# Windowed attention with a mixture of experts on one core: half of a slot's row split and one weight split moved into the next step, the slot's rows requested ahead of a step's last loads, a quarter of some q and k loads issued from GpSimd

## The chip, the cores and the metric

One core of a Trainium2 chip runs the whole kernel. The time is device microseconds of one execution; three runs of the kernel before gave 609.14, 609.82 and 610.5 us, median 609.82. The engines are TensorE (PE, with its weight loads PEld), VectorE (DVE), ScalarE (ACT), GpSimd (POOL) and SyncE (SP, which here only issues DMAs). Each engine runs its own instructions in the order in which the program wrote them, and waits where one depends on another engine.

## The reference

The inputs are q, k and v of shape (8 batches, 8 heads, 576 positions, 64), the weights of 8 experts and a gate. Attention sees a causal window of 64 positions; its output becomes 4608 rows of 512, and each row goes to one expert.

```python
scores = scale * np.matmul(q, k.transpose(0, 1, 3, 2))
scores = np.where((rel >= 0) & (rel < 64), scores, -1e9)   # rel = pos_q - pos_k
attn = exp(scores - max); attn /= attn.sum() + 1e-9
x = (attn @ v) as rows of 512
logits = x @ w_gate + modality_bias[modality_id]
e_idx = argmax(logits); gate_w = softmax(logits)[e_idx]
out[mask] = gate_w[mask] * (relu(x[mask] @ w1[e]) @ w2[e])    # for each expert e
```

## The kernel before, in words

**Steps.** The attention is worked off in 36 pieces of 128 rows (two blocks of 64), one step `s` each, in the loop at line 1080 that runs to `s` = 39. A step holds several stages of different pieces: `values(s - 2)` (probabilities times v, and on DVE `values_out`, which divides by the sums and writes `xa`, L726), `logits(s - 3)` (the gate's matmuls, L744, and the addition of the bias on DVE, L749, which also frees the PSUM bank), `scores(s)` (L659), `minima(s)` (eight DVE instructions that mask and take the row's minimum, L673), the transposing of the probabilities of piece `s - 1` on PE with copies on ACT (`probs_t`, L694), the exponentials on ACT (`exps`, L685, in three groups: two, three and three of the eight heads), the transposing of `xa` for the gate (`x_t`), the routing, and `part(0)` and `part(1)`, which bring the next group's q or k into transposed form.

**Order.** The schedule is manual: instructions stand on each engine in the order of the program. Work that is to stand a little later is appended to the list `later`, and `run_later()` empties it.

**Slots of the experts.** Rows whose expert is known are scattered to `xs_scratch` in HBM by GpSimd (L828). From step 12 on, slots of 256 rows of one of two chosen experts are computed between the attention's stages: a generator, `slot_pieces`, yields one piece of work after the other, and `gap` takes one. A slot has 16 pieces and a step takes four, so a slot lasts four steps. The pieces are twelve for k = 1 to 3 (two of `first`, x times w1, L321; two of `second`, h times w2, L343), then `second(3, 0)` of the old slot, `first(0, 0)` and `first(0, 1)` of the next one, and `second(3, 1)` of the old one. With the slots beginning at step 12, these last four lie in the steps with s % 4 == 0 (16, 20, 24, 28, 32, 36).

**A slot's rows.** In the fourth gap of a step with s % 4 == 2 `fetch` reads the slot's row number into SP's register (L204) and asks for the rows with five DMAs on SP (L217); they must wait for the scatters that write these rows. A step later, behind the second gap, `x_turn` transposes them on DVE (two instructions, L283). Then the rows are split into a high part (`xh`, cast on ACT, L195) and a remainder (`xl`, subtraction on DVE, L196), in two halves: `x_part(nxt, 0)` and `x_part(nxt, 1)`. `x_part` itself emits no work: it appends the split, and for the second half also two small GpSimd copies (gate and id, L304 and L306), to `later`. Before the change both are emitted at the end of the step with s % 4 == 3, around the last piece of that step. Each group of `first` has 12 matmuls: the first six use the first half of the channels, the last six the second, and the remainder `xl` is used last in each six.

**Weights.** The two experts' weights come in 32 pieces of 256 KB, from step 5 to about step 25. `weights(s)` splits the remainder of the piece before (`split_lo` on DVE, L119), casts the next piece's high part (`split_hi` on ACT, L114), and asks SP for another piece (L103, L107).

**Loads of q and k.** `load_qk` issues one group's loads. In the groups of `WHOLE` (10, 12, 14, 16, 17) every head goes directly to the layout that DVE transposes (`turn_heads`, L585): per head two DMAs of 32 KB, each of 32 rows with 8 runs of 128 bytes. k of group G is loaded in step 2G - 3 and transposed in step 2G - 2, q one step later each. Of these DMAs, a quarter (odd heads, second half) is issued from ACT's queue, the rest from SP's (L608): 40 in all, 20 of k and 20 of q. In a step the loads are called in four places: `loads(3)`, `loads(1)`, `loads(1)` and at the end `loads(9)`, which takes what is left; in a `WHOLE` group that is the last two heads. `loads(9)` stands ahead of the fourth gap, hence of `fetch`.

**GpSimd.** In a step it copies the lower half of v (`swap_v`, L551), which `values` needs a step later, adds the small number to the sums (L700), scatters two pieces of rows in every second step, and scatters a finished slot's output (L354).

Of the kernel before, what the change touches and what calls it, by code (L numbers as in the profile page):

```python
# [26 lines left out]
def tile_window_attn_moe(  # L27
# [12 lines left out]
    nc = tc.nc  # L40
# [88 lines left out]
    def tick(n=1, table=False):  # L129
        for _ in range(n):  # L130
            if routing and not table:
                routing.pop(0)()
            elif queue:
                queue.pop(0)()
                issued[0] += 1
# [105 lines left out]
    RAWS = 8  # L241
    fetched = []
    later = []
    scattered = []

    n_tps = [0]
# [14 lines left out]
    def run_later():  # L261
        while later:
            later.pop(0)()
# [21 lines left out]
    def slot_pieces():  # L285


        def x_part(sl, i):

            xt, nb = sl["xt"], sl["nb"]  # L290
            if nb == 1:
                return
            if i == 0:
                sl["x"] = [epool.tile([P, NC1 * TP], F32R, name=nm) for nm in ("xh", "xl")]
            cs_ = slice(2 * i, 2 * i + 2)
            raw = x_of(xt).rearrange("p b w c t -> p c (b w) t")[:, cs_]
            hi, lo = (x[:, cs_.start * TP:][:, 0:512].rearrange("p (c w t) -> p c w t", w=2 * NR, t=R32)
                      for x in sl["x"])

            def out_():  # L300
                split(raw, hi, lo)
                if i == 1:
                    sl["gate"] = epool.tile([P, 2], F32, name="gate", bufs=2)
                    nc.gpsimd.tensor_copy(out=sl["gate"], in_=tail_of(xt)[:, :, 0])  # L304
                    sl["id"] = epool.tile([P, 2], I32, name="id", bufs=2)
                    nc.gpsimd.tensor_copy(out=sl["id"], in_=tail_of(xt)[:, :, 1])  # L306
            later.append(out_)
# [118 lines left out]
        while True:  # L426
            nxt = None
            for k in range(1, NK):
                for i in range(2):
                    if k == 1 and i == 0 and last:  # L430
                        nxt = fetch()
                        turn_at = 0
                    first(sl, k, i)
                    if k == NK - 1 and i == turn_at:
                        later.append(lambda: x_turn(nxt))
                    yield
                for t in range(2):
                    if k == 2 and t == 1 and nxt is None:
                        nxt = fetch()
                        turn_at = 1  # L440
                    second(sl, k - 1, t)
                    if k == NK - 1 and nxt and t == 1 and nxt["nb"] == 2:
                        x_part(nxt, 1)
                    yield
                    if k == NK - 1 and nxt and t == 0:
                        x_part(nxt, 0)
                        run_later()
            if nxt["nb"] == 1:
                break
            second(sl, NK - 1, 0)  # L450
            yield
            first(nxt, 0, 0)
            yield
            first(nxt, 0, 1)
            yield
            second(sl, NK - 1, 1)
            yield
            sl = nxt
# [130 lines left out]
    def load_qk(G, nm, blocks=range(GBLK), dma=nc.sync, hs=range(H)):  # L589

        t = qk[G, nm]
        x = q if nm == "q" else k
        nh = n_plain(G)
        i = blocks[0]
        while i <= blocks[-1]:
            b, g = divmod(GBLK * G + i, BPB)
            n = min(BPB - g, blocks[-1] + 1 - i)
            p0 = i * W64 // 2
            for par in range(2 if hs[0] < nh else 0):
                src = x[b, 0:nh, g * W64:(g + n) * W64].rearrange("h (p t) d -> p t h d", t=2)  # L600
                dma.dma_start(out=plain(t, nh)[p0:p0 + n * W64 // 2, par], in_=src[:, par])  # L601
            u = slice(i * W64 // R32, (i + n) * W64 // R32)
            for h in hs if hs[0] >= nh else ():
                for c in range(2):
                    rows = slice((h % 2 * 2 + c) * R32, (h % 2 * 2 + c + 1) * R32)
                    src = x[b, h, g * W64:(g + n) * W64, c * R32:(c + 1) * R32]
                    other = nh == 0 and h % 2 and c
                    (nc.scalar if other else dma).dma_start(  # L608
                        out=by_heads(t, nh)[rows, (h - nh) // 2, u, :],
                        in_=src.rearrange("(u p) d -> p u d", p=R32))  # L610
            i += n
# [108 lines left out]
    def values_out(p):  # L720
        rs = st.pop((p, "rs"))
        rw = small.tile([P, 2, 2, HP], F32, name="rw")
        nc.vector.reciprocal(
            out=rw, in_=rs.rearrange("p (c g) -> p g c", g=2)[:, :, None, :].broadcast_to([P, 2, 2, HP]))
        xa = st[p, "xa"] = xas[p % XBUF]
        nc.vector.tensor_tensor(  # L726
            out=xa[:, 0:DM].rearrange("p (x d) -> p x d", d=R32),
            in0=st.pop((p, "av")).rearrange("p h d -> p (h d)").rearrange("p (x d) -> p x d", d=R32),
            in1=rw.rearrange("p g a c -> p (g a c)")[:, :, None].broadcast_to([P, 2 * H, R32]), op=ALU.mult)
# [334 lines left out]
            out=wg[c * R32:(c + 1) * R32],  # L1064
            in_=w_gate[c * P:(c + 1) * P].rearrange("(r d) e -> d r e", d=R32))

    def weights(s):

        if halves:
            split_lo(*halves.pop(0))  # L1070
        n = 2 if s < FIRST + 4 else 1
        if len(raws) >= n or raws and not pieces:
            split_hi(*raws[0])
            halves.append(raws.pop(0))
        while pieces and len(raws) < n:
            x, c = pieces.pop(0)
            raw = epool.tile([P, WCH], F32, name="y", bufs=4)
            raws.append((load_piece(raw, evs[x], c), x, c))

    for s in range(NPR + 4):  # L1080
# [10 lines left out]
        def loads(n):  # L1091

            for f, args in at.get(s, [])[:n]:
                f(*args)
            at[s] = at.get(s, [])[n:]
# [31 lines left out]
                route1((s - 3) // GB)  # L1127
        if FIRST < s < NPR + 2:
            values_out(s - 2)
        if s < NPR:  # L1130
            scores(s)
            if s == FIRST:
                x_turn(fetched[0])
                gap(it, True)
            minima(s)
            if s == FIRST - 2:
                tick(todo[0][-1] - issued[0], table=True)
# [58 lines left out]
        if s == WEIGHTS:  # L1196
            load_weights()
        if s >= WEIGHTS:
            weights(s)
        if s > FIRST:  # L1200
            loads(9)
        if n_gap > 3:
            gap(it, True)
        run_later()
        if s == 1:
            select_bias()
        if s == 4:
            nc.sync.dma_start(out=xs_blk[DUMMY:DUMMY + 2].rearrange("b p c -> p b c"), in_=padrow)
        for T, xs_ in EARLY:
            if T == R:  # L1210
                plan(T, xs_, cnt)
    tick(len(routing))
    release()
    tick(len(queue))
# [132 lines left out]
    while next(it, "end") != "end":  # L1347
# [20 lines left out]
        if swaps and swaps[0][0] <= t:  # L1368
# [4 lines left out]
            else:  # L1373
                split_hi(raw, buf, c)
                split_lo(raw, buf, c)
    assert not swaps and not todo
    manual.__exit__(None, None, None)
    actx.close()

# [124 lines left out]
```

## Time and profile before

| | |
|---|---|
| runs | 609.14, 609.82, 610.5 us (median 609.82) |
| the profiled execution | 611.84 us, span 610.0 us, granted TensorE clock 0.997 |
| busy: PE, DVE, ACT, POOL | 96%, 62%, 46%, 23% of the span |
| DMA queues: SP's (q1), GpSimd's (q0), ACT's (q10) | 66.02, 18.92 and 1.89 MB |
| steps 12 to 35 (74.5 to 313 us) | PE busy 231.9 of 238.5 us |

The page has the busy time of each engine, the span in 40 slices, the chain of work that ended last and the costliest groups. In a timeline each row has the start, the duration, engine, line, operation, what is written and read, and in brackets the engine's idle time before it and what ended it. `SPq` and `ACTq` are those engines' DMA issues. "x9" is the number of instructions merged in a row. Instructions of one engine overlap by a few hundredths, so the start of the next is where the one before ended, for this purpose.

### The profile page before, as it was taken

How to read it: one execution, taken by the hardware profiler on the slowest of the kernel's cores; microseconds unless marked ns; L12 is line 12 of the kernel's file. 1: busy time of each engine (PE TensorE's matmuls, PEld its weight loads, DVE VectorE, ACT ScalarE, POOL GpSimd, SP SyncE). 2: the span in 40 equal slices, each digit the busy share in tenths (PEclk: the TensorE clock that was granted, in tenths of full speed). 3: DMA queues.
4: the chain of work that ended last, by engine and by line, in shares of the span. 5: the costliest groups of instructions: out<-in, count | busy, mean ns of one | idle time of the engine just before them, and what ended most of it. 6: DMA issues, size and time to landing. Idle time of an engine off the chain costs nothing.

```text
span 610.0 us, 17261 instructions
## 1 busy us (share of the span) xinstructions
PE 588.4 (96%) x6241; PEld 522.5 (86%) x6241; DVE 377.0 (62%) x1479; ACT 282.8 (46%) x907; POOL 138.4 (23%) x313
## 2 busy tenths in 40 slices
PE   7999889999899999999999999999999999999996
PEld 4888788889689898889898899899999999999983
DVE  4889988887767877768756465323224634765311
ACT  3999876665556655555562211111113522553110
POOL 6332322142132312321323131011001111102102
PEclk9999989999999999999999999999999999999999
DMA  9989867685865846554713033632152553687401
GB/s 169 212 226 246 212 180 168 144 196 133 203 155 132 229 88 155 145 107 86 188 54 105 36 105 127 188 102 70 36 174 77 166 174 103 194 255 215 153 23 38
DMA packets 186855, 87.95 MB, mean 144 GB/s; under 512 B 151002, under 2 KB 169488, under 8 KB 186640
## 3 DMA queue, kind: packets, MB, share of 16 engines
q1 hardware_dynamic: 167312, 66.02, 44.8%
q0 software_dynamic: 5840, 18.92, 8.2%
q10 hardware_dynamic: 13616, 1.89, 1.8%
q8 instruction: 50, 0.82, 0.6%
q14 instruction: 37, 0.30, 0.2%
HBM read 67.36 MB, written 23.78 MB: 149 GB/s over the span
## 4 chain that ended last, share of the span: by engine, by line
PE 76%; DVE 9%; DMA 6%; ACT 3%; issue 2%; POOL 2%; SPq 1%; POOLq 0%; DVEq 0%; ACTq 0%
PE y L343 29%; PE em L321 20%; PE sp L321 10%; PE tp L483 6%; PE av L715 4%; PE sp L659 3%; DVE ss L673 2%; DMA qk<-in_k_dram 2%; DMA xs_scratch<-xa,idx 2%; PE tp L744 2%; ACT ss L685 1%; DMA xt<-xs_scratch 1%; DVE xl L196 1%; POOL xs_scratch L828 1%; SPq L601 1%
## 5 line engine op out<-in xcount | busy, mean ns | idle before, releaser
L343 PE MATMUL y<-Whi,hh 128*128 128x512 f32 x288 | 115.8, 402 | 0.0
L685 ACT ACTIVATE ss<-ss,mn 128x128 f32<-128x128 f32 x288 | 112.2, 397 | 3.8 <-DMA wg<-in_moe_w_gate_dram 2.7
L343 PE MATMUL y<-Wlo,hh 128*128 128x512 f32 x288 | 112.7, 391 | 0.0
L343 PE MATMUL y<-Whi,hl 128*128 128x512 f32 x288 | 112.4, 390 | 0.0
L330 DVE SCALAR_TENSOR_TENSOR hl<-em,hh 128x512 fp32r<-128x512 f32 x50 | 34.6, 691 | 91.3 <-ACT hh L329 91.2
L354 POOL DMA_INDIRECT out_dram<-y,id x36 | 38.6, 1073 | 217.7 <-DVE y L351 160.1
L321 PE MATMUL em<-xh,Whi 128*128 128x256 f32 x400 | 82.1, 287 | 0.0
L321 PE MATMUL em<-xh,Wlo 128*128 128x256 f32 x400 | 79.5, 280 | 0.0
L321 PE MATMUL em<-xl,Whi 128*128 128x256 f32 x400 | 79.5, 280 | 0.0
L329 ACT ACTIVATE hh<-em 128x512 fp32r<-128x512 f32 x50 | 29.9, 598 | 105.1 <-PE em L321 100.2
L321 PEld LDWEIGHTS em<-xh,Whi 128*128 128x128 f32 x400 | 63.2, 190 | 2.3
L343 PEld LDWEIGHTS y<-Whi,hl 128*128 128x128 f32 x288 | 54.1, 188 | 12.1
L673 DVE CUSTOM_DVE_ANT_0 ss<-sp,masks 128x128 f32<-128x128 f32 x288 | 63.4, 285 | 1.5 <-PE sp L659 1.5
L694 ACT COPY pT<-tp 128x512 f32<-128x512 f32 x57 | 31.3, 589 | 70.9 <-PE tp L483 70.7
L343 PEld LDWEIGHTS y<-Whi,hh 128*128 128x128 f32 x288 | 54.1, 188 | 9.5 <-issue 0.8
L343 PEld LDWEIGHTS y<-Wlo,hh 128*128 128x128 f32 x288 | 54.2, 188 | 8.5
L321 PEld LDWEIGHTS em<-xl,Whi 128*128 128x128 f32 x400 | 61.4, 189 | 0.0
L321 PEld LDWEIGHTS em<-xh,Wlo 128*128 128x128 f32 x400 | 61.4, 189 | 0.0
L828 POOL DMA_INDIRECT xs_scratch<-xa,idx x36 | 36.3, 1009 | 89.3 <-DVE e_n_p L154 23.5
L685 ACT ACTIVATION_READ_ACCUMULATOR ss<-ss,mn 128x1 f32 x288 | 56.1, 195 | 0.0
L329 ACT ACTIVATE hh<-sp 128x512 fp32r<-128x512 f32 x22 | 13.1, 597 | 80.4 <-PE sp L321 80.4
L715 PEld LDWEIGHTS av<-ve,pT 128*64 128x64 f32 x576 | 36.3, 138 | 13.1 <-issue 6.9
(239 smaller groups left out, 1131.5 us busy)
## 6 DMA issues: line engine op xcount, KB each, us to landing
xt<-xs_scratch SPq DMA_DIRECT2D x72, 128.0 KB
vo<-in_v_dram SPq DMA_DIRECT2D x32, 256.0 KB
y<-in_moe_w_dram SPq DMA_DIRECT2D x32, 256.0 KB
vo<-in_moe_w_dram SPq DMA_DIRECT2D x18, 256.0 KB
ss<-in_moe_w_dram SPq DMA_DIRECT2D x18, 256.0 KB
xs_scratch<-xs_scratch SPq DMA_DIRECT2D x8, 514.0 KB
pT<-in_moe_w_dram SPq DMA_DIRECT2D x12, 256.0 KB
qk<-in_k_dram SPq DMA_DIRECT2D x76, 32.0 KB
```

The costliest lines, as they stand in the source:

```text
L321: nc.tensor.matmul(out=hb[:, i * TP:(i + 1) * TP], lhsT=w[buf][:, c0:c0 + P], rhs=x[:, c * TP:(c + 1) * TP], start=(n == 0), stop=(n == le ...
L329: nc.scalar.activation(out=hh, in_=hb, func=AF.Relu),
L330: nc.vector.scalar_tensor_tensor(out=hl, in0=hb, scalar=0.0, in1=hh.bitcast(F32), op0=ALU.max, op1=ALU.subtract)))
L343: nc.tensor.matmul(out=sl["y", t], lhsT=h[:, i * TP + t * P:i * TP + (t + 1) * P], rhs=w[buf][:, c0:c0 + DM], start=(k == 0 and n == 0), s ...
L354: ins = nc.gpsimd.indirect_dma_start(out=out, out_offset=bass.IndirectOffsetOnAxis(ap=sl["id"][:, t:t + 1], axis=0), in_=y, in_offset=None ...
L483: nc.tensor.transpose(out=out_, in_=in_, identity=ident[p0:p0 + n, p0:p0 + n])
L659: nc.tensor.matmul(out=sp[a][c * W64:(c + 1) * W64, hp * P:(hp + 1) * P], lhsT=qT[rows, place(g + c, hp), :], rhs=kT[rows, win(c, hp), :], ...
L673: nc.vector.tensor_tensor_reduce(out=ss[a][:, hp, :], in0=sp[a][:, hp * P:(hp + 1) * P], in1=mask, scale=-1.0 / 8.0, scalar=3.0e38, op0=AL ...
L685: nc.scalar.activation(out=ss[a][:, hp, :], in_=ss[a][:, hp, :], func=AF.Exp, bias=mn[:, h:h + 1], scale=-1.0, accum_out=sm[:, h:h + 1])
L694: nc.scalar.copy(out=pT, in_=pp)
L715: nc.tensor.matmul(out=by_block(av)[c * W64:(c + 1) * W64, a, :, hp, :], lhsT=pT[:, i:i + W64], rhs=(vo if c else ve)[p][:, 2 * hp + a, :] ...
L828: ins = nc.gpsimd.indirect_dma_start(out=xs, out_offset=bass.IndirectOffsetOnAxis(ap=idx[:, j:j + 1], axis=0), in_=xg[j], in_offset=None)
```

## The change

`x_part(nxt, 1)` is no longer called where the step with s % 4 == 3 ends. It is put into a new list, `splits`, which the next step empties behind `values_out` and ahead of `scores`. In the phase behind the steps (when `last` is set) it is called at once, as before. In steps with s % 4 == 3 beyond step 12 the last call of `weights` puts its `split_lo` into the same list. `loads(9)` stands behind the fourth gap. The quarter of the `WHOLE` groups' loads goes to GpSimd's queue instead of ACT's.

```diff
--- before.py
+++ after.py
@@ -241,6 +241,7 @@
     RAWS = 8
     fetched = []
     later = []
+    splits = []
     scattered = []
 
     n_tps = [0]
@@ -439,8 +440,10 @@
                         nxt = fetch()
                         turn_at = 1
                     second(sl, k - 1, t)
-                    if k == NK - 1 and nxt and t == 1 and nxt["nb"] == 2:
-                        x_part(nxt, 1)
+                    if k == NK - 1 and nxt and t == 1:
+                        splits.append(lambda: x_part(nxt, 1))
+                        if last:
+                            splits.pop(0)()
                     yield
                     if k == NK - 1 and nxt and t == 0:
                         x_part(nxt, 0)
@@ -605,7 +608,7 @@
                     rows = slice((h % 2 * 2 + c) * R32, (h % 2 * 2 + c + 1) * R32)
                     src = x[b, h, g * W64:(g + n) * W64, c * R32:(c + 1) * R32]
                     other = nh == 0 and h % 2 and c
-                    (nc.scalar if other else dma).dma_start(
+                    (nc.gpsimd if other else dma).dma_start(
                         out=by_heads(t, nh)[rows, (h - nh) // 2, u, :],
                         in_=src.rearrange("(u p) d -> p u d", p=R32))
             i += n
@@ -1064,9 +1067,12 @@
             out=wg[c * R32:(c + 1) * R32],
             in_=w_gate[c * P:(c + 1) * P].rearrange("(r d) e -> d r e", d=R32))
 
-    def weights(s):
-
-        if halves:
+    def weights(s, late=False):
+
+        if halves and late:
+            half = halves[0]
+            splits.append(lambda: (halves.remove(half), split_lo(*half)))
+        elif halves:
             split_lo(*halves.pop(0))
         n = 2 if s < FIRST + 4 else 1
         if len(raws) >= n or raws and not pieces:
@@ -1127,6 +1133,8 @@
                 route1((s - 3) // GB)
         if FIRST < s < NPR + 2:
             values_out(s - 2)
+        while splits:
+            splits.pop(0)()
         if s < NPR:
             scores(s)
             if s == FIRST:
@@ -1196,12 +1204,12 @@
         if s == WEIGHTS:
             load_weights()
         if s >= WEIGHTS:
-            weights(s)
-        if s > FIRST:
-            loads(9)
+            weights(s, s > FIRST and s % 4 == 3)
         if n_gap > 3:
             gap(it, True)
         run_later()
+        if s > FIRST:
+            loads(9)
         if s == 1:
             select_bias()
         if s == 4:
@@ -1209,6 +1217,8 @@
         for T, xs_ in EARLY:
             if T == R:
                 plan(T, xs_, cnt)
+    while splits:
+        splits.pop(0)()
     tick(len(routing))
     release()
     tick(len(queue))
@@ -1373,7 +1383,7 @@
             else:
                 split_hi(raw, buf, c)
                 split_lo(raw, buf, c)
-    assert not swaps and not todo
+    assert not swaps and not todo and not splits
     manual.__exit__(None, None, None)
     actx.close()
```

## The prediction

> **What bounds the kernel now.** I read the page first, then the windows by step, the waits of PE between 100 and 330 us (there the change acts), and the timelines of PE, DVE, ACT, SP and POOL around the steps that begin a new slot.
>
> ```profile
> PE 588.4 (96%) x6241; PEld 522.5 (86%) x6241; DVE 377.0 (62%) x1479; ACT 282.8 (46%) x907; POOL 138.4 (23%) x313
> ```
>
> PE lacks 610.0 - 588.4 = 21.6 us of being busy throughout, which caps any gain.
>
> ```profile
> 157.27:171.19 13.92, 11.13 (x141) 9.46 (x137) 11.12 (x44) 8.09 (x26) 5.02 (x11) 1.00 0.79 212
> 201.20:212.93 11.73, 10.90 (x141) 9.47 (x137) 9.67 (x44) 6.92 (x24) 4.57 (x9) 1.00 0.90 237
> 242.96:253.79 10.83, 10.67 (x140) 9.48 (x136) 8.76 (x42) 5.92 (x23) 3.49 (x6) 1.00 0.56 147
> ```
>
> These are steps 20, 24 and 28, each counted from its score matmuls: the stretch, its length, then busy time of PE, PEld, DVE, ACT and POOL. A step with s % 4 == 0 finishes one slot and begins the next. Step 20 leaves PE idle for 2.79 us, step 24 for 0.83, step 28 for 0.16. The waits say who was late:
>
> ```profile
> PE tp L483 <- DVE lg L749: 2.4, 4, 0.9
> PE sp L659 <- DVE qT L585: 1.7, 1, 1.7
> ```
>
> Four times a transposing of probabilities waits for the logits' addition on DVE (it frees the bank), once the scores wait for a transposed q. PE's rows give the places (bracket: idle before):
>
> ```profile
> 119.30 0.66 PE L483 MATMUL tp<-ident_r,ss 128*128 128x128 f32 x4 [0.43 <-DVE lg L749]
> 159.59 0.67 PE L659 MATMUL sp<-kT,qT 64*64 64x128 f32 x16 [1.66 <-DVE qT L585]
> 161.76 0.66 PE L483 MATMUL tp<-ident_r,ss 128*128 128x128 f32 x4 [0.91 <-DVE lg L749]
> 203.50 0.65 PE L483 MATMUL tp<-ident_r,ss 128*128 128x128 f32 x4 [0.61 <-DVE lg L749]
> 323.44 0.66 PE L483 MATMUL tp<-ident_r,ss 128*128 128x128 f32 x4 [0.40 <-DVE lg L749]
> ```
>
> So steps 16, 20, 24 and 36 lose 0.43 + 1.66 + 0.91 + 0.61 + 0.40 = 4.01 us to DVE, and steps 28 and 32 nothing. About 4 us is what the change can reach. Why DVE is late at step 20:
>
> ```profile
> 154.28 0.69 DVE L330 SCALAR_TENSOR_TENSOR hl<-em,hh 128x512 fp32r<-128x512 f32 x1 [0.68 <-ACT hh L329]
> 157.12 1.30 DVE L283 STREAM_TRANSPOSE xt<-xt 128x512 f32<-128x512 f32 x2 [2.15 <-DMA xt<-xs_scratch]
> 158.85 0.69 DVE L585 STREAM_TRANSPOSE qT<-qk 128x512 f32<-128x512 f32 x1
> 159.46 0.96 DVE L119 TENSOR_TENSOR Wlo<-y,Whi 128x512 fp32r<-128x512 f32 x1
> 160.34 1.28 DVE L196 TENSOR_TENSOR xl<-xt,xh 128x512 fp32r<-128x512 f32 x2
> 161.55 0.15 DVE L749 TENSOR_TENSOR lg<-tp,bias_sel 128x8 f32<-128x8 f32 x1
> 164.28 0.42 DVE L557 COPY ve<-vo 64x512 f32<-64x512 f32 x1
> ```
>
> DVE stood 2.15 us waiting for the slot's rows, then ran without a break from 157.12 to 164.70. The rows were late because of SP:
>
> ```profile
> 141.17 7.44 SPq L608 DMA_DIRECT2D qk<-in_q_dram  x9
> 148.85 1.26 SPq L103 DMA_DIRECT2D y<-in_moe_w_dram  x1
> 150.16 1.42 SPq L608 DMA_DIRECT2D qk<-in_q_dram  x3
> 152.53 2.45 SPq L217 DMA_DIRECT2D xt<-xs_scratch  x5
> ```
>
> **The change, part by part.**
>
> *Rows asked sooner.* At steps 18, 22, 26 and 30 the fetch now stands before the last loads (those of `loads(9)`) on SP. From 152.53, the three loads (1.42 with their gaps 1.47) go behind: rows asked at 151.06. What is now queued behind the fetch's waits (its row number, the scatter's landing) is these three loads and the next step's loads. They come 0.95 + 2.45 = 3.4 us later at most, so end by 155.0, where the second q transposing now runs at 158.85. That hides them.
>
> *A quarter of the loads on GpSimd.* 40 loads of 32 KB leave ACT's queue. SP's nine loads took 7.44 us, 0.83 each; its three took 0.47 each. Nine at 0.47 are 4.2 us, so 3.2 us of the stretch is waiting. For what:
>
> ```profile
> SPq L608 <- DMA qk<-in_k_dram: 13.2, 7, 3.4
> SPq L608 <- DMA qk<-in_q_dram: 10.2, 7, 3.0
> 142.03 0.32 ACTq L608 DMA_DIRECT2D qk<-in_q_dram  x1
> ```
>
> SP's loads wait for landings of other loads, up to 3.0 us at a time; ACT issues its quarter among its exponentials, the first at 142.03, inside SP's stretch. If SP waits for those, moving them frees SP 3.2 us earlier, at 147.9 rather than 151.1 with the reordering. Then the rows wait for the scatter that writes them. At the next fetch the pair of scatters, the first issued at 187.42, had landed 4.74 us later:
>
> ```profile
> 187.42 4.74 DMA xs_scratch<-xa,idx
> 143.52 1.06 POOL L828 DMA_INDIRECT xs_scratch<-xa,idx  x1 [7.28 <-DVE kT L585]
> ```
>
> The pair of step 18 begins at 143.52, so it lands at about 148.3. The rows, which took 157.12 - 152.53 = 4.59 us from the request, are there at 152.9, before 154.97, when DVE is free. The whole 2.15 us goes; with the reordering alone, 1.47.
>
> By the Trainium skill, "DMA: Bandwidth & Descriptors", section "Issuing engines are not separate DMA queues", DMAs from all engines interleave on the same 16 engines, and issuing from several saves only the sequencers' issue time. By it SP would gain nothing, since SP issues as many loads as before, and the step would win 1.47; the 23.4 us that SP's loads waited speak against it.
>
> What a load costs POOL isn't in this trace. Its bounds:
>
> ```profile
> L951 POOL DMA_DIRECT2D brow<-n_moe_modality_bias_dram x1 | 0.7, 745 | 0.0
> 231.19 0.98 POOL L828 DMA_INDIRECT xs_scratch<-xa,idx  x1 [0.76 <-POOL xa L827]
> L551 POOL COPY ve<-vo 64x512 f32<-64x512 f32 x36 | 22.8, 634 | 34.0 <-DMA vo<-in_v_dram 30.1 <-PE av L715 1.6 <-PE tp L744 1.1
> ```
>
> The first is a plain load into 128 partitions, the second a scatter of 128 rows. One of the moved loads has 256 pieces of 128 bytes: 0.75 us if their number counts for nothing, 2 x 0.98 = 2.0 if it is the whole cost. I take 1.1, nearer the plain load. Four in a step are 4.4 us, beside the 3.5 of 10.8 for which POOL is busy in step 28. The tight place is step 26, where the scatters end at 231.19 + 0.98 = 232.17 and the q loads now follow:
>
> ```profile
> 241.46 0.27 PE L715 MATMUL av<-ve,pT 128*64 128x64 f32 x1
> 242.34 0.71 DVE L585 STREAM_TRANSPOSE qT<-qk 128x512 f32<-128x512 f32 x1
> ```
>
> At 1.1 us the fourth is issued by 236.6. With some 2.4 us to land (an estimate, half of the scatter pair's 4.74) it is there at 239.0, 3.3 before its transposing. The `ve` copy behind it (0.63) ends at 237.2, 4.2 before its matmuls. So it costs nothing; that cover is gone at (242.34 - 232.17 - 2.4) / 4 = 1.9 us a load. What ACT gains, 40 issues of 0.3 to 0.4 us, falls in steps where PE never waits for ACT: nothing.
>
> *The splits.* `splits` runs before the scores, but `x_part` only appends to `later`, which is next emptied behind the first piece of slot work. So the second half's `xh` and `xl` do not come right behind the logits: on DVE `xl` follows the minima and the `ve` copy, on ACT `xh` follows the first two exponentials. The weight's remainder (three of them: steps 15, 19, 23) goes where it says, behind `xa`. The logits' addition comes 0.64 (half of 1.28) sooner, with the weight's remainder 1.3 or more. All four waits on `lg` vanish. But the new slot's first group needs the second half from its 7th matmul (`xh`) and 11th (`xl`) on. In DVE's unbroken run the sum of work is the same, so `xl` now ends where `ve` ended:
>
> ```profile
> 121.82 0.42 DVE L557 COPY ve<-vo 64x512 f32<-64x512 f32 x1
> 122.34 0.40 PE L321 MATMUL em<-xl,Whi 128*128 128x256 f32 x2
> 206.02 0.43 DVE L557 COPY ve<-vo 64x512 f32<-64x512 f32 x1
> 206.56 0.40 PE L321 MATMUL em<-xl,Whi 128*128 128x256 f32 x2
> ```
>
> - Step 16: `xl` ends near 122.24; PE, 0.43 early, wants it at 121.91 and waits until about when it ran before (122.34). Net 0.
> - Step 24: it ends near 206.45, and PE ran there at 206.56. Net 0.
> - Step 20: everything moves with the rows, by 2.15.
> - Step 36: no minima or exponentials, `xl` is early: +0.4.
>
> Steps 28 and 32 had no wait to remove:
>
> ```profile
> 246.10 0.40 ACT L685 ACTIVATE ss<-ss,mn 128x128 f32<-128x128 f32 x1
> L195 ACT CAST xh<-xt 128x512 fp32r<-128x512 f32 x36 | 20.5, 617 | 7.0 <-DVE se L814 4.5 <-DVE xt L283 2.5
> 247.00 0.39 PE L321 MATMUL em<-xh,Whi 128*128 128x256 f32 x2
> 247.47 0.40 PE L321 MATMUL em<-xl,Whi 128*128 128x256 f32 x2
> ```
>
> ACT's two exponentials follow PE's transposes and end at 246.5; `xh` (20.5 / 36 = 0.57) ends at 247.1, wanted at 247.00. `xl` (0.64) follows until 247.75, wanted at 247.47: PE loses 0.3, and 0.3 again in step 32, which has the same order. The last boundary, behind step 39, has idle ACT and DVE: 0.
>
> *Sum.* 2.15 + 0.4 + 0 + 0 - 0.3 - 0.3 = 1.95 us. The profiled execution takes 611.84 us (span 610.0, 1.84 around it), hence 609.9. The median of the runs is 609.82, 2.02 lower; the same step from it gives 607.9, -0.32%. A difference under 0.2%, 1.2 us, can hardly be told from none.
>
> **Rivals.**
>
> 1. *SP isn't relieved* (the rule above): step 20 gains 1.47, the sum is 1.3, 608.5. For it: the rows don't say that it is ACT's loads SP waits for. Against: the waits of 3.0 us. 0.14, half of it beyond 0.2%.
> 2. *The second half is late everywhere.* If `xl` misses its matmuls by 0.8 in steps 16, 20, 24, 28 and 32 beyond what I counted (say ACT's `xh` waits behind more), 0.4 x 5 = 2.0 go, and nothing is left: 609.8. For it: PE has no slack. Against: the same DVE work in the same span. 0.21, no difference.
> 3. *The second half is never missed*: 0.43 and 0.61 come back in steps 16 and 24, and the 0.6 isn't lost: 3.6, so 606.2. Against: DVE has no gap there. 0.06.
> 4. *POOL becomes the bound.* Over 1.9 us a load, the last q load of steps 18, 22, 26, 30 and 32 is late by four times the excess, and the next scores wait for `qT`. At 2.5 us that is 5 x 2.4 = 12 us, less 2: about 620; at 2.1, 4 less 2: 612. For it: 2.0 is one of the two bounds, and POOL's scatters wait ahead of the q loads. Against: the plain load's 0.75. 0.17, slower.
>
> **The numbers.** The forecast has 0.42, all beyond 0.2%. Faster is 0.42 + 0.07 + 0.06 = 0.55, same 0.07 + 0.21 = 0.28, slower 0.17. The range reaches from rival 3 to 611.2, the near edge of rival 4; outside it lies most of rival 4 and little else.
>
> **What would show it.** Right: no wait before the `xt` transposes near 155; the steps 20 to 21 apart by about 11.7 instead of 13.92; no wait of `tp` on `lg`; instead waits of `em` (L321) on `xh` or `xl` of 0.2 to 1.0; the rows' request near 148 to 149; POOL loads near 1.1 us. Wrong: POOL loads near 2 us with `qT` waits behind them; step 20 unchanged; `em` waits of 0.8 in every boundary.

## The result, and the profile after

| | kernel before | changed kernel |
|---|---|---|
| median (range), 5 runs each | 609.82 us (608.93 to 610.50) | 613.53 us (612.37 to 615.57) |
| the profiled execution: time, span | 611.84, 610.0 us | 612.37, 610.6 us |

The changed kernel is 0.66% slower: ratio 1.0066, 95% interval 1.0043 to 1.0089. The forecast was 0.32% faster. Repeated on three chips with more runs, the loss was 0.27%, 0.36% and 0.24% (under the experiments): the loss is there, but the size of the first comparison did not come back.

The page's busy line:

```profile
PE 590.6 (97%) x6241; PEld 523.8 (86%) x6241; DVE 377.2 (62%) x1479; ACT 282.7 (46%) x907; POOL 163.6 (27%) x353
```

GpSimd has 40 instructions and 25.2 us more. TensorE is 2.2 us busier with the same number of instructions; DVE and ACT are as they were. Steps 20, 24 and 28 by the windows view, columns as in the prediction:

```profile
156.96:168.50 11.54, 11.20 (x140) 9.63 (x136) 8.75 (x36) 6.84 (x24) 5.75 (x11) 1.00 0.77 212
198.50:212.03 13.53, 11.66 (x141) 9.59 (x137) 10.46 (x44) 8.20 (x26) 5.09 (x11) 1.00 0.87 226
242.05:253.27 11.22, 11.19 (x141) 9.62 (x137) 8.87 (x42) 6.34 (x23) 3.58 (x6) 1.00 0.53 139
```

Step 20 fell from 13.92 to 11.54 us, as forecast. Step 24 rose from 11.73 to 13.53, where the forecast had no change, and took back three quarters of it. Step 28 has hardly an idle moment on TensorE (11.19 of 11.22 us busy) and is still 0.39 longer. TensorE's waits between 100 and 330 us:

```profile
PE em L322 <- DVE xl L196: 1.1, 3, 0.4
PE em L322 <- ACT xh L195: 0.8, 1, 0.8
PE tp L486 <- DVE lg L752: 0.6, 1, 0.6
```

Three of the four waits on `lg` are gone, and the wait on `qT`; waits for the moved half, `xl` and `xh`, have come. The chain behind step 24, from the timeline (line numbers of the changed kernel are up to 3 higher here):

```profile
186.73 0.99 POOL L831 DMA_INDIRECT xs_scratch<-xa,idx  x1 [0.65 <-POOL xa L830]
...
191.99 2.45 SPq L217 DMA_DIRECT2D xt<-xs_scratch  x5
194.49 1.45 SPq L611 DMA_DIRECT2D qk<-in_q_dram  x3
196.21 0.36 SPq L107 DMA_DIRECT2D y<-in_moe_w_dram  x1
...
199.05 0.62 ACT L114 CAST Whi<-y 128x512 fp32r<-128x512 f32 x1 [2.40 <-DMA y<-in_moe_w_dram]
199.58 0.61 ACT L195 CAST xh<-xt 128x512 fp32r<-128x512 f32 x1
200.22 0.69 DVE L196 TENSOR_TENSOR xl<-xt,xh 128x512 fp32r<-128x512 f32 x1 [1.07 <-ACT xh L195]
...
201.05 0.66 PE L486 MATMUL tp<-ident_r,ss 128*128 128x128 f32 x4 [0.58 <-DVE lg L752]
204.57 0.50 PE L322 MATMUL em<-xh,Whi 128*128 128x256 f32 x2 [0.78 <-ACT xh L195]
205.74 0.50 PE L322 MATMUL em<-xl,Whi 128*128 128x256 f32 x2 [0.43 <-DVE xl L196]
```

And the same places before:

```profile
194.44 2.46 SPq L217 DMA_DIRECT2D xt<-xs_scratch  x5
197.17 0.35 SPq L107 DMA_DIRECT2D y<-in_moe_w_dram  x1
...
200.03 0.62 ACT L114 CAST Whi<-y 128x512 fp32r<-128x512 f32 x1 [0.68 <-DMA y<-in_moe_w_dram]
```

Read it downwards. SP stands at the fetch until 191.99, for the scatter of 186.73, which lands at 191.8, 5.07 us after its issue. Behind the rows come the three q loads, and only then, at 196.21, the weight piece that ScalarE casts next: 2.29 us before step 24's scores (198.50), against 201.20 - 197.17 = 4.03 in the kernel before. ScalarE waits 2.40 for it; its queue holds the rows' cast `xh` behind that, DVE's `xl` waits for `xh`, and the logits' addition stands behind `xl`.

The program's end is later too. The last scatter and the span, first after, then before (timeline of GpSimd's last microseconds):

```profile
core 0 of [0], span 610.6 us
...
605.36 1.05 POOL L408 DMA_INDIRECT out_dram<-y,id  x1 [1.98 <-DVEq L1392]
```

```profile
core 0 of [0], span 610.0 us
...
605.95 1.06 POOL L407 DMA_INDIRECT out_dram<-y,id  x1 [1.99 <-DVEq L1382]
```

The last scatter is issued 0.59 us earlier and the span ends 0.6 later: from the scatter 5.24 us instead of 4.05. In the trace's sequencer records that is GpSimd's closing instruction (0.74 instead of 0.40) and the drain behind it (2.55 instead of 1.66).

### The profile page after: what moved, and what is told of

Same layout as the page of the kernel before. It is cut to its first block, busy times and chain, and to the rows that moved or that the text cites. A ratio compares the mean times of both kernels' runs of the same rounds, so it can differ in the third digit from the quotient of the medians.

```text
span 610.6 us, 17316 instructions
## 1 busy us (share of the span) xinstructions
PE 590.6 (97%) x6241; PEld 523.8 (86%) x6241; DVE 377.2 (62%) x1479; ACT 282.7 (46%) x907; POOL 163.6 (27%) x353
## 4 chain that ended last, share of the span: by engine, by line
PE 80%; DVE 4%; ACT 2%; issue 1%; DMA 0%; POOL 0%; POOLq 0%; DVEq 0%; ACTq 0%
PE y L344 30%; PE em L322 22%; PE sp L322 10%; PE tp L486 7%; PE av L718 4%; PE sp L662 3%; PE tp L747 2%; DVE ss L676 1%; DVE xt L284 1%; ACT ss L688 1%; PE tp L394 1%; PE em L369 1%; DVE Wlo L119 0%; DMA y<-in_moe_w_dram 0%; DVE xl L196 0%
```

## The experiments

Theory A is the chain above: the three q loads and the weight piece queue behind the fetch's wait for the scatter, the piece comes late, and step 24 pays. Its rivals are D (GpSimd's loads delay the scatter), C and S (the moved half itself costs, or costs nothing), and G and L (the clock, of the program or by luck). P, Q and B are rivals of single runs; R, T and U came later, for the end and the late scatter.

Each kernel was timed in 7 to 12 runs beside 17 to 35 of the kernel before on the same chip, whose median there was between 611.0 and 613.0 us. The table has the ratio to it, and lengths in us from the profiled execution: steps 20, 24, 28 and 32, from step 35's scores to the last matmul, and from there to the end.

| kernel | ratio (95%) | 20 | 24 | 28 | 32 | 35 to last | end |
|---|---|---|---|---|---|---|---|
| kernel before | | 13.92 | 11.73 | 10.83 | 9.57 | 291.94 | 5.41 |
| c0_before | 1.0017 (1.0002, 1.0031) | 13.69 | 11.60 | 10.82 | 10.33 | 292.25 | 5.46 |
| changed, first | 1.0066 (1.0043, 1.0089) | 11.54 | 13.53 | 11.22 | 10.08 | 291.34 | 6.52 |
| r_after | 1.0027 (1.0013, 1.0042) | 12.16 | 13.26 | 11.22 | 10.08 | 291.34 | 6.33 |
| r2_after | 1.0036 (1.0021, 1.0050) | 12.13 | 13.55 | 11.21 | 10.66 | 292.38 | 6.70 |
| r3_after | 1.0024 (1.0005, 1.0042) | 12.01 | 13.61 | 11.22 | 10.08 | 291.34 | 6.33 |
| p_order: reordering alone | 0.9987 (0.9975, 0.9998) | 11.91 | 11.88 | 10.83 | 10.10 | 292.27 | 5.76 |
| p_pool: GpSimd loads alone | 1.0007 (0.9996, 1.0019) | 11.84 | 11.50 | 10.93 | 10.24 | 292.35 | 6.46 |
| p_splits: splits alone | 1.0008 (0.9994, 1.0023) | 13.39 | 11.39 | 11.22 | 10.64 | 292.51 | 5.73 |
| u_order: all but the reordering | 0.9997 (0.9980, 1.0015) | 11.46 | 12.06 | 11.22 | 10.08 | 291.34 | 6.46 |
| u_pool: all but the GpSimd loads | 1.0000 (0.9982, 1.0018) | 11.66 | 12.30 | 11.22 | 10.08 | 291.66 | 5.76 |
| op: all but the splits | 0.9996 (0.9982, 1.0011) | 11.94 | 12.51 | 10.86 | 9.57 | 291.94 | 6.33 |
| wp22 | 1.0012 (0.9999, 1.0025) | 11.74 | 11.92 | 11.21 | 10.72 | 292.16 | 6.39 |
| pool80 | 0.9991 (0.9980, 1.0002) | 11.53 | 11.56 | 11.22 | 10.09 | 292.15 | 5.58 |
| shift38 | 0.9997 (0.9980, 1.0015) | 13.17 | 11.56 | 11.22 | 10.08 | 291.34 | 6.13 |
| best | 0.9961 (0.9941, 0.9981) | 12.54 | 11.52 | 10.82 | 10.23 | 292.24 | 5.41 |
| best_again | 0.9968 (0.9949, 0.9988) | 12.03 | 11.47 | 10.83 | 9.57 | 291.34 | 5.40 |
| best38 | 0.9998 (0.9980, 1.0015) | 12.48 | 11.55 | 10.85 | 9.57 | 291.51 | 6.13 |
| best18 | 0.9968 (0.9954, 0.9981) | 12.48 | 11.48 | 10.84 | 9.57 | 291.34 | 5.58 |

Rows of one program show how far an execution's draw goes: step 20 by 0.6 us, step 32 by 0.8, the part from step 35 by 1.0. Steps 24 and 28 repeat to 0.35 and 0.01. A difference in step 32 or from step 35 on that is below these is not told from a draw.

**The control, `c0_before`: no edit.**

> The kernel before, unchanged, run as if it were a changed one. Theory G (the granted TensorE clock differs from program to program): its five executions all have a clock of 0.996 or more and agree with the kernel before within 0.2%, while the changed kernel's five had 0.988 to 0.993. Theory L (the clock differs from execution to execution by luck): its five spread over 0.988 to 0.997 like the changed kernel's, and the time goes with them, by 0.3 to 0.6 us for each 0.001 of clock.

The clocks of its 12 runs spread from 0.987 to 0.998, the times from 611.98 to 616.40, so the clock differs from execution to execution, as theory L has it and G has not. But L's second half fails: the time doesn't follow the mean clock run by run (613.45 us at 1.000 among the runs of the kernel before). And the same program comes out 0.17% slower than itself: a ratio within 0.2% of 1 says little here, and step lengths say more.

**The parts alone.** `p_order` moves `loads(9)` only, `p_pool` has only `nc.gpsimd` for `nc.scalar` in `load_qk`, `p_splits` only the list `splits`:

```diff
-        if s > FIRST:
-            loads(9)
         if n_gap > 3:
             gap(it, True)
         run_later()
+        if s > FIRST:
+            loads(9)
```

> Only the reordering: the last loads of a step behind the fetch. Theory A (the three q loads and the weight piece queue behind the fetch's wait for the scatter at step 22, and ScalarE's cast of the piece comes late at step 24): step 20 shorter by about 1.5 us (13.9 to 12.4), step 24 longer by 1.2 to 1.8 (11.7 to 13.0 or more) with PE waiting for lg and em there, steps 28 and 32 unchanged; the sum is within 0.5 us of the kernel before, 609.3 to 610.3. Rival D (it is the GpSimd loads that delay the scatter's landing): step 24 unchanged here, the sum -1.5, 608.3.

> Only the quarter of loads on GpSimd's queue. Theory A: SP's loads end sooner, rows of step 20 asked 1 to 2 us sooner, step 20 shorter by 1.0 to 2.2; step 24 unchanged within 0.3, since nothing new stands behind the fetch; about 608.3. Rival D: the scatter of step 22 lands later behind the GpSimd loads, the rows and the weight piece with it, step 24 longer by 0.5 or more. Rival P (the queue of GpSimd, 25 us busier, costs elsewhere): slower than the kernel before by over 1 us, 611 or more.

> Only the moved splits (half of the rows' and three of the weight's remainder). Theory C (the second half comes late for its matmuls): steps 16, 28 and 32 longer by 0.2, 0.4 and 0.5 us with waits of em on xl or xh, step 20 unchanged or longer by up to 0.5, step 24 within 0.3; the sum +0.8 to +1.5, 610.6 to 611.3. Rival G: slower by 2.5 or more with the clock of all executions at 0.993 or less, although the steps account for 1 us only. Rival S (the splits cost nothing, the loss is in the queues): within 0.4 us of the kernel before.

Step 24 was not longer, neither with the reordering alone (11.88; theory A wanted 12.9 or more) nor with the GpSimd loads alone (11.50; rival D wanted 12.2 or more). Either brings the whole gain of step 20, 1.9 and 2.0 us. `p_splits` shows theory C's price at step 28, +0.39; its price at steps 16 and 32 and the shorter step 20 are inside the draws, and the sum, 0.4 us by the medians, is half of the 0.8 that C wanted at least. `p_pool` shows the end 1 us later, which none of the theories had; of the 1.5 us that theory A expected of this part, the medians show 0.2.

**All but one part**, with the changed kernel again:

> The changed kernel unchanged, beside the kernel before on one chip. Theory A (the sum of the places seen in the traces: step 20 -2.3 us, step 24 +1.85, steps 28 and 32 +0.4 each, step 36 -0.6, and GpSimd's end of program +1.0): 0.5 to 1.0 us slower than the kernel before. Theory G (something of the whole program that these places don't show, seen as half clock in the first 15 us): 2.5 us or more slower again, with a mean clock of 0.992 or less against 0.993 for the kernel before. Rival L (much of the 3.7 us was the draw of the executions): within 0.5 us either way.

> The changed kernel with the last loads put back ahead of the fetch: splits and GpSimd loads remain. Theory A: step 24 returns to 11.4 to 11.6 us, since the q loads and GpSimd's loads are no longer behind the scatter; step 20 stays near 11.5, steps 28 and 32 stay 0.4 longer, the end of the program stays 1 us longer; about 1.0 us faster than the kernel before. Rival D (GpSimd's loads on the scatter's queue delay it): step 24 stays at 13 or more.

> The changed kernel with the quarter of loads back on ScalarE's queue: reordering and splits remain. Theory A: the end of the program returns to 5.4 to 5.8 us behind the last matmul (6.5 in the changed kernel), step 20 at 11.5 to 12.0; step 24 at 13 or more if the reordering alone puts the weight piece behind the wait, steps 28 and 32 0.4 longer; within 0.5 us of the kernel before. Rival D: step 24 at 11.4 to 11.6, about 1.5 us faster than the kernel before.

> The changed kernel without the splits: reordering and GpSimd loads together. Theory A: step 20 at 11.5 to 11.9, step 24 at 13 or more as in the changed kernel (neither part alone did this: 11.88 and 11.50), steps 28 and 32 as in the kernel before, the end of the program +1.0: within 0.6 us of the kernel before. Rival C (the moved half makes step 24 late): step 24 at 11.5 to 11.9, about 1 us faster than the kernel before.

The changed kernel is slower again, by 2.3 us. Each of the three with one part undone comes back to the time of the kernel before, and to a step 24 between 12.06 and 12.51. No theory had that: A wanted 13 or more in `op`, and in `u_order` 11.4 to 11.6. So no part alone lengthens step 24 beyond its draw, each pair does by 0.4 to 0.8 us, and all three by 1.8. The reordering and the GpSimd loads together make the piece late: it is asked 2.6 us before step 24's scores in `op`, against 3.8 with the reordering alone and 4.2 with the GpSimd loads alone. In `op` TensorE pays at the logits' addition:

```profile
201.26 0.66 PE L483 MATMUL tp<-ident_r,ss 128*128 128x128 f32 x4 [1.40 <-DVE lg L749]
```

With the splits moved as well, this wait is 0.58, since only one of the two `xl` still stands ahead of the addition; but the moved half then comes late itself, and TensorE waits 0.78 and 0.43 for it (the rows of 204.57 and 205.74 above) and is busy for 0.8 us longer. Together the splits add 1.0 (13.5). The end is 6.3 to 6.7 in all kernels with 40 GpSimd loads and 5.4 to 5.8 with none.

**Is it the late weight piece?** `wp22` is the changed kernel, but asks for two pieces in step 22, so that SP has the next one out ahead of the fetch:

```diff
-        while pieces and len(raws) < n:
+        while pieces and len(raws) < (2 if s == 22 else n):
```

> The changed kernel a second time, as the neighbour of the next three kernels, and to see how far two loadings of one program differ. Its step 24 at 13.2 to 13.6 us again; 1 to 2.5 us slower than the kernel before.

> The changed kernel, but step 22 asks for two weight pieces instead of one, so that the piece that step 23 would ask for stands ahead of the fetch and its wait. Theory A (the late weight piece holds up ScalarE, and the rows' cast behind it): ScalarE no longer waits for the piece (2.40 us in the changed kernel), step 24 falls from 13.4 to 12.0 or less, the time by 1.3 to 2.0 us against the changed kernel. Rival Q (the three q loads behind the rows, or the later rows themselves, are what is late): step 24 stays at 12.8 or more. Rival S (the second half of the split is late whatever the weights do): em waits of 0.7 or more remain in step 24.

The pieces and ScalarE's casts in the timeline of `wp22`:

```profile
183.83 0.98 SPq L107 DMA_DIRECT2D y<-in_moe_w_dram  x2
...
196.35 0.61 ACT L114 CAST Whi<-y 128x512 fp32r<-128x512 f32 x1
197.61 0.62 ACT L195 CAST xh<-xt 128x512 fp32r<-128x512 f32 x1 [0.66 <-DVE se L817]
```

No wait for the piece; the rows' cast begins 0.68 us before step 24's scores (198.29 in this kernel) instead of 1.08 behind them (199.58 and 198.50). Step 24 is 11.92 instead of 13.55, and the time 0.9 us below its neighbour `r2_after` by the medians, less than the step's 1.6 and than the 1.3 that was expected at least. The q loads and the rows stood within 0.2 us of where they had stood, so rival Q falls. Of the waits for the moved half 0.07 and 0.42 remain in step 24, below the 0.7 of rival S.

**Why did the scatter land late, and why does the end cost 1 us?** First the number of loads, `pool80`:

```diff
-                    other = nh == 0 and h % 2 and c
+                    other = nh == 0 and c
```

> The changed kernel with all second halves of these heads' loads on GpSimd's queue, 80 loads instead of 40. Theory T (GpSimd's end of program grows with the number of loads it has issued: last matmul to end 5.4 to 5.8 us with none, 6.3 to 6.5 with 40): 7.2 to 7.6 here. Rival U (a fixed price for having plain loads there at all): 6.3 to 6.6. GpSimd's loads at 0.605 us each, eight in a step 4.8 us; step 24 at 13.5 or more, as the scatter's landing is later still; 1.5 to 4 us slower than the kernel before.

Both theories of the end fall, and so does rival D: with eight loads behind the scatter instead of four, it lands 3.86 us after its issue, step 24 is 11.56, and the end is back:

```profile
core 0 of [0], span 609.4 us
...
605.17 1.06 POOL L408 DMA_INDIRECT out_dram<-y,id  x1 [1.98 <-DVEq L1392]
```

4.23 us from the last scatter to the end. The expectation of 1.5 to 4 us slower was wrong too: the time was that of the kernel before. What singles out the scatter of step 22 in the changed kernel is the bracket in the row of 186.73 above: 0.65 us behind the small copy, where second scatters of a step stand 0.28 behind it. In the kernel before the same thing is in a row that the prediction shows, the scatter of 231.19 with 0.76. Counting the DMAs ahead of these two on GpSimd's queue, a scatter and the program's first load as 1 each and a moved load as a half, gives 28 for both. It is so in every execution in which a second scatter stands at 28: 0.65 in the eight with 40 loads, 0.76 in the eight with none. `pool80` has one with 0.64 at count 62:

```profile
269.93 1.00 POOL L831 DMA_INDIRECT xs_scratch<-xa,idx  x1 [0.64 <-POOL xa L830]
```

The changed kernel ends at 94, `pool80` at 114, the kernel before at 74. This suggested theory R: a place that returns every 33 or 34, whatever stands on it. `shift38` moves it off the scatter with two loads:

```diff
+                    kept = G == 10 and nm == "k" and h < 4
-                    (nc.gpsimd if other else dma).dma_start(
+                    ((nc.scalar if kept else nc.gpsimd) if other else dma).dma_start(
```

> The changed kernel a third time, as the neighbour of the next kernel: step 24 at 13.2 to 13.6 us, last matmul to end 6.3 to 6.7, 1.5 to 2.3 us slower than the kernel before.

> The changed kernel with two of the 40 loads (k of the group loaded in step 17, heads 1 and 3) back on ScalarE's queue, so that every later DMA of GpSimd's queue moves up. Theory R (the price sits at a place that comes back in this queue: counting a scatter as 1 and such a load as a half, at 28 and 62 and at the end of the program at 94, in all traces so far; the changed kernel has the second scatter of step 22 at 28 and its end at 94): step 22's second scatter is issued 0.28 us behind the copy before it instead of 0.65 and lands about 1 us sooner, step 24 falls to 12.2 or less, last matmul to end to 5.4 to 5.8; 1.5 to 2.5 us faster than the changed kernel. Rival D (the loads behind the scatter delay it; there are as many as in the changed kernel): step 24 stays at 13.2 or more. Rival U (a price for plain loads on this queue): the end stays at 6.3 or more.

Its timeline:

```profile
187.09 0.99 POOL L832 DMA_INDIRECT xs_scratch<-xa,idx  x1 [0.28 <-POOL xa L831]
188.07 2.42 POOL L612 DMA_DIRECT2D qk<-in_q_dram  x4
...
190.89 2.44 SPq L217 DMA_DIRECT2D xt<-xs_scratch  x5
...
197.89 0.62 ACT L114 CAST Whi<-y 128x512 fp32r<-128x512 f32 x1 [0.50 <-DMA y<-in_moe_w_dram]
```

With the same four loads behind it, the scatter has its 0.28 again; the rows are asked 3.80 us behind its issue (190.89 - 187.09) instead of 5.26 (191.99 - 186.73), ScalarE waits 0.50 for the piece instead of 2.40, and step 24 is 11.56. So theory R holds for the place at 28. At the end it fails: 6.13, not 5.4 to 5.8, with a count of 93. Nor is the return at 62 borne out: in `shift38` a second scatter stands at 62 too, without a delay, and the same in `best38`:

```profile
328.40 0.98 POOL L832 DMA_INDIRECT xs_scratch<-xa,idx  x1 [0.28 <-POOL xa L831]
```

By the medians `shift38` is 1.4 us faster than `r3_after`, just below the expected 1.5. It gave 1.2 us back in step 20, which nobody expected: ScalarE waits there 2.42 us for a weight piece, asked behind the wait of the fetch one slot earlier, in step 18, whose scatter took 4.69 us to land.

**A version from the parts that pay.** `best` has the reordering, two pieces asked in step 22, and the splits except at two boundaries; the quarter of loads stays on ScalarE's queue (the main lines, against the kernel before):

```diff
+                        splits.append(lambda: x_part(nxt, 1))
+                        if last or s in (27, 31):
+                            splits.pop(0)()
...
+        while pieces and len(raws) < (2 if s == 22 else n):
```

> A version from the parts that pay: the kernel before with the last loads behind the fetch, two weight pieces asked in step 22, the splits moved except at the boundaries of steps 28 and 32, and the quarter of loads left on ScalarE's queue. Theory A: step 20 at 11.5 to 11.9 (13.7 to 13.9 before), step 24 at 11.3 to 11.7, step 28 at 10.83, step 36 0.3 to 0.6 shorter, the end of the program as before: 2.0 to 2.8 us faster than the kernel before, a ratio of 0.9955 to 0.997. Rival L (loadings of one program differ by 0.2%): anything from 0.994 to 0.999 is then no contradiction; over 0.999 says that the sum misses something.

> The version from the parts that pay, a second time: 0.25 to 0.5% faster than the kernel before if its 0.39% was not the draw of one loading; within 0.2% if it was.

> The version from the parts that pay, with 38 loads on GpSimd's queue. Theory A with R (GpSimd's loads relieve SP and cost nothing where the queue's place falls on no waited-for scatter): step 20 at 11.5 to 11.8 against 12.5 without them, the end at 5.4 to 5.8; 0 to 1 us faster than the version without. If the loads have a price of their own, it is slower than that version.

> The version from the parts that pay, with two weight pieces asked in step 18 as well as in step 22. Theory A (the piece behind the fetch's wait also delays ScalarE at step 20: 1.07 us in the version without): no such wait at step 20, which falls from 12.0 to 12.5 to 11.4 to 11.6 us; 0.4 to 1.0 us more of a gain, 2.2 to 3.2 us faster than the kernel before. Rival B (the extra piece's buffer or bandwidth delays another load in steps 18 to 20): step 20 unchanged or longer.

`best` beats both kernels twice, the kernel before by 0.39% and 0.32%: 1.6 and 1.9 us by the medians, below the expected 2.0 to 2.8, because step 20 is 12.0 to 12.5 and not 11.5 to 11.9. Steps 20, 24 and 28 of `best_again`:

```profile
157.66:169.68 12.02, 11.19 (x140) 9.61 (x137) 8.95 (x36) 7.29 (x25) 4.99 (x11) 1.00 0.79 215
199.68:211.15 11.47, 11.18 (x141) 9.62 (x137) 9.47 (x44) 6.86 (x24) 4.56 (x11) 1.00 0.85 233
241.19:252.01 10.82, 10.65 (x140) 9.48 (x136) 8.82 (x42) 5.93 (x23) 3.49 (x6) 1.00 0.56 145
```

All three are at or below the kernel before, and step 20 still has 0.8 us. `best38`, with 38 loads on GpSimd, gave the gain back: its end is 0.7 later and step 20 no shorter, so these loads have a price of their own, as the expectation's other branch had it. `best18` missed: ScalarE's wait for the piece is gone in step 20, but the extra piece stands ahead of the fetch on SP, the rows come later (DVE waits 0.94 us for them), and step 20 is 12.48 (rival B); the gain is 1.4 us, not 2.2 to 3.2.

## Why the prediction was wrong

Its sum went by places, so it can be checked by places. Means over the four profiled executions of the changed kernel less the two of the kernel before:

| place | forecast | measured |
|---|---|---|
| step 20 | -2.15 | -1.84 |
| steps 14 to 19 (with step 16) | 0 | 0.0 |
| step 24 | 0 | +1.82 |
| step 28 | +0.3 | +0.39 |
| step 32 | +0.3 | +0.28 |
| from step 35 | -0.4 | -0.50 |
| end of the program | not in the sum | +1.04 |
| sum | -1.95 | +1.2 |

The values for step 32 and from step 35 on lie within the draws of one program.

- **Step 20** was right in place and nearly in size. The rows are asked earlier and DVE no longer waits for them. The forecast gave the reordering alone 1.47 of it and the loads the rest; measured, the reordering alone gave -1.9, the GpSimd loads alone -2.0, both -1.84. One of its readings was off without harm: the 4.74 us in the row of 187.42 is the first scatter's landing, the second landed at 193.0, 5.6 us after the pair began.
- **The failed step** is "That hides them". It listed "these three loads and the next step's loads" as what is queued behind the fetch's waits, put the lateness at 3.4 us at most and compared it with one reader, the second q transposing. The list leaves out the next weight piece, whose cast stands ahead of the rows' cast on ScalarE. In step 22 SP stands at the fetch for 7.5 us (184.48 to 191.99), until the scatter has landed, and the piece is asked 2.29 us before the scores of step 24 instead of 4.03. `wp22` moves that piece alone, and step 24 gets 1.6 us shorter. The wait could be seen in the kernel before, in step 20, where the piece is asked 2.0 us before the scores and DVE is not the only engine that is late:

```profile
158.20 0.62 ACT L114 CAST Whi<-y 128x512 fp32r<-128x512 f32 x1 [2.81 <-DMA y<-in_moe_w_dram]
158.72 1.13 ACT L195 CAST xh<-xt 128x512 fp32r<-128x512 f32 x2
```

- **"So it costs nothing"**, of GpSimd's loads, was right for their own durations and wrong for the queue. The view by groups has them at

```profile
L611 POOL DMA_DIRECT2D qk<-in_q_dram x20 | 12.1, 626 | 0.0
L611 POOL DMA_DIRECT2D qk<-in_k_dram x20 | 12.1, 618 | 0.3
```

  0.62 us each, below the forecast's 1.1 and below its lower bound of 0.75; rival 4 never came near. But the 12 loads that are issued up to then bring the second scatter of step 22 to the late place at count 28, and that scatter is what the fetch of step 22 waits for. And the end of the program, which the sum left out, is 1.0 us later with 40 loads; why stays open.
- **"Net 0" for step 24** also had `xl` end where the `ve` copy ended. That holds only when `xh` is in time; here the late piece cost 1.0 us more with the splits than without them (13.5 against 12.5 in `op`). Rival 2 named that mechanism, "ACT's `xh` waits behind more", for five boundaries; a wait of 0.8 us for `xh` came at this one alone.
- **Steps 28 and 32** were right: the moved half comes late for its matmuls (for step 32, the draw of 0.6 to 0.8 us leaves the size open). The last matmul of the first half and those of the moved half in the changed kernel's step 28, then the weight loads of two of them:

```profile
245.86 0.40 PE L322 MATMUL em<-xl,Whi 128*128 128x256 f32 x2
246.24 0.50 PE L322 MATMUL em<-xh,Whi 128*128 128x256 f32 x2
246.58 0.40 PE L322 MATMUL em<-xh,Wlo 128*128 128x256 f32 x2
246.97 0.50 PE L322 MATMUL em<-xl,Whi 128*128 128x256 f32 x2
246.24 0.30 PEld L322 LDWEIGHTS em<-xh,Whi 128*128 128x128 f32 x2 [0.19 <-ACT xh L195]
246.97 0.30 PEld L322 LDWEIGHTS em<-xl,Whi 128*128 128x128 f32 x2 [0.19 <-DVE xl L196]
```

  The matmuls start 0.38, 0.34 and 0.39 apart, where the prediction's two rows of this group, 247.00 and 247.47, are 0.47 apart over two steps, 0.23 each. No bracket of PE shows it; those of PEld do, 0.19 for `xh` and 0.19 for `xl`, 0.38 in all. TensorE's matmuls overlap these waits, so 0.4 us are lost with hardly any idle time.
- **Rival 1** (SP isn't relieved) fell as a sum: the GpSimd loads alone shorten step 20 by 2.0 us, although SP issues as many loads as before. The two rows of 13.2 and 10.2 us, SP's waits for other loads, are gone in `p_pool` and in the changed kernel. By the traces' semaphore records SP's and ScalarE's DMAs take turns on the same eight semaphores, and GpSimd's have eight of their own: in the kernel before, SP's load of 145.19 waits for the semaphore of ScalarE's load of 142.03.

The places give +1.2 us, the three repeats +2.3, +2.1 and +1.1 by their medians. Of the first comparison's 3.7 us the rest isn't settled. Its five runs of the changed kernel had clocks of 0.988 to 0.993, mean 0.990, the repeats means of 0.993 to 0.995; for the kernel before in that comparison no clocks were recorded. A draw of half-clock stretches (below) fits, but was not shown for those runs.

## What to carry to other kernels

When a transfer that waits is moved ahead in an issuing queue, list everything behind it up to the next wait, follow each to its reader and that reader's own queue, and do it for every step in which it happens: the price here was a weight piece, which another engine reads than the loads that were moved. Undo one part at a time, since two parts that each gain can lose together. Where two loadings of one program (placed on the chip anew) differ by 0.2%, compare lengths of steps before times: here 16 to 19 of the 23 steps from 12 to 34 repeat within 0.05 us, though most of those that begin a slot do not.

## What the runs showed of the hardware

**A late place in GpSimd's queue.** At count 28 a second scatter was issued 0.37 us late with GpSimd loads and 0.48 without, in all 16 executions that had one there, and at count 62 in `pool80` 0.36 late, but not at all at count 62 in `shift38` and `best38`; that the place returns is not shown. Step 22's second scatter, where it stood at 28 with four loads behind it, took 4.98 to 5.10 us from issue to landing (three executions of the changed kernel and `u_order`), against 3.67 to 4.66 at other counts. The place alone doesn't make it slow: step 26's second scatter, at 28 with no loads behind it, landed in 3.46 to 3.85 us (`p_splits`, `u_pool`, `best_again`, `best18`), and landings of 4.9 us and more came at other counts too. What lengthens the landing stays open. The end was dear at 93 and 94 (6.1 to 6.7 us) and cheap at 74 and 114 (5.4 to 5.8). By the Trainium skill, "DMA: Bandwidth & Descriptors", section "SWDGE vs HWDGE vs iDMA", GpSimd appends its DMAs' descriptors to descriptor rings. A ring that begins anew could make one place late; no run here shows that this is the cause.

**Half clock by draw.** `best` and `best_again` are one program; their first 20 us by the windows view (the granted clock is the third number from the right):

```profile
0.00:20.00 20.00, 16.92 (x204) 11.13 (x204) 11.57 (x68) 10.73 (x41) 11.43 (x57) 1.00 0.94 179
```

```profile
0.00:20.00 20.00, 17.05 (x184) 12.27 (x188) 10.32 (x65) 9.72 (x37) 10.02 (x54) 0.83 0.89 169
```

The second has 6.83 us of half clock from 8.7 us on, and 20 matmuls fewer done by 20 us. Of 19 profiled executions six had this, two had 3.41 us, and four had 3.41 us near 81 us, behind the 1.8 us or more for which TensorE idles in step 12. Steps 0 to 11 took 67.0 us on average with the 6.83 us (66.4 to 68.2) and 66.2 without any (65.7 to 66.8): some 0.8 us on average, in ranges that overlap. By the Trainium skill, "TensorE: Matmul & The Clock Gate", Part 1, the gate's window is 3413 ns and runs freely, not from the kernel's start; stretches of 3.41 and 6.83 us that come and go in one program agree with that.
